# Gating the turns of the next batch by the MoE position, K ahead of Q, and a later zeroing

## The chip, the cores and the metric

One core of one Trainium2 chip. The metric is device time in microseconds (us) of one execution. Every time quoted is the median of several runs; most executions of a kernel here lie within 1% of their median. The engines are named as in the profile: PE (TensorE), ACT (ScalarE), DVE (VectorE), POOL (GpSimd) and SP (SyncE; SPq is its DMA queue). The granted clock, as the profile reads it, is the share of its full clock at which PE could run. "Chunk n" is the n-th group of 64 rows of the sequence, nine chunks to a batch, 72 in all.

## The reference

Cut to what matters: windowed attention over 8 batches of 8 heads, 576 positions and 64 values per head; its result, reordered to 4608 tokens of 512 values, goes through a two-layer block with a squared ReLU (called MoE in the code).

```python
scores = (q @ k.transpose(0, 1, 3, 2)) / np.sqrt(64)
mask = np.abs(pos[:, None] - pos[None, :]) <= 32
attn = softmax(np.where(mask, scores, -1e9))
x = (attn @ v).transpose(0, 2, 1, 3).reshape(4608, 512)
h = x @ w_in                       # 512 x 2048
r = np.maximum(h, 0.0)
out = (r * r) @ w_out              # 2048 x 512
```

## The kernel before

The program records every operation with its engine, what it reads and writes, a modelled duration and a key. A list scheduler written in Python then runs through modelled time; on each engine it issues the ready operation with the lowest key. What it decides is the order on each engine; the waits are semaphores and run on the chip's own time.

```python
def rec(self, eng, fn, reads=(), writes=(), dma=None, dur=100, key=0.0, move=0, after=(), old=()):
    ...                                   # after: operations that must be scheduled earlier
def schedule(self):
    ...
        t, e = best                       # the engine that can issue first, in modelled time
        while wait[e] and wait[e][0][0] <= t:
            _, i, op = heapq.heappop(wait[e])
            heapq.heappush(pool[e], (op.key, i, op))
        op = heapq.heappop(pool[e])[2]    # lowest key among the ready ones
    ...
```

Batches 0 and 1 are turned (transposed) on PE. From batch 2 on, GpSimd loads Q and K raw, VectorE turns them into a staging tile (1.3 us for 512 columns, 1.6 us for 640), and SyncE's queue carries the staging tiles to their places (the "spread"). There is one staging tile for Q and one for K, and two raw tiles of each. So the last Q turn of batch b frees the raw Q tile, and the Q load of batch b+2 can start then (that of batch 4 started 2.0 us after the turn's end in the kernel before, at 85.67 us, and 0.3 us after it in the changed one, at 86.16 us).

```python
def turn(self, b, t, dh, m0, m1, key, after):
    raw, st, i = self.RAW[t][b % 2], self.ST[t], b % 2
    ...
    self.p.rec("DVE", lambda e: e.transpose(dst, src),
               reads=[("raw", t, i, g) for g in range(4)], writes=[("st", t, dh, m0)], key=key,
               dur=40 + 312 * n, after=after)

def spread(self, b, t, key):              # K: 4 transfers of 144 KB, Q: 8 of 72 KB, on SP
    for dh in range(2):                   # two halves, each after two of the four turns
        ...
def copy_v(self, b, key, s0, s1):         # two transfers of 264 KB on SP, vx<-vd
    ...
# in build(), for b > 1
    for st in range(8):
        t, dh, m = ("q", "k")[st // 4], st // 2 % 2, st % 2
        self.turn(b, t, dh, 5 * m, 5 + 4 * m, 9 * b - LEAD - TOFF + st * TST + (5 if b == 2 else 0),
                  [self.masked[min(9 * b - TREL + st, 9 * b - 1) if b > 2 else 12 + st // 2]])
        if st % 4 == 3:
            self.spread(b, t, 9 * b - LEAD - 9)
    self.copy_v(b, 9 * b - LEAD - 6, 0, 4)
```

In the profile the transposes appear as `kst<-kraw` and `qst<-qraw`, the spreads as `kt<-kst` and `qz<-qst`, the V copies as `vx<-vd`. The first scores of a batch (`sc<-qz,kt`) need all of both spreads. Behind the scores come the product with V (`avp`, A·V), its scaling on DVE (`xr`), the transpose of that on PE (`trp`, `xt`) and the MoE (`ht`, its square `gt`, `outp`).

The softmax here doesn't subtract the row's maximum and nothing guards it: scores larger than these inputs give would overflow.

## Time and profile before

| | before |
|---|---|
| median of 3 runs | 346.15 us (343.3 to 348.79) |
| span of the profiled run | 345.2 us |
| PE busy | 312.3 us, 90% |
| PE waits between 60 and 170 us | 9.0 us |
| granted clock in that profile | 0.97 |

The prediction below shows the page, the stretches and the waits. One more view belongs here, since it matters later: the timeline of the kernel before around the first scores of batch 2. The columns are start, length, engine and line, operation, tiles, count, and in brackets the idle time of the engine just before and what ended it. A line of several instructions gives the length from the first to the last.

```profile
89.25 6.18 SPq L378 DMA_DIRECT2D kt<-kst  x4
...
91.81 1.32 DVE L366 STREAM_TRANSPOSE kst<-kraw 128x512 bf16<-128x512 bf16 x1
93.43 2.40 POOL L307 DMA_DIRECT2D kraw<-in_k_dram  x4 [4.75 <-DVE gt L497]
...
101.07 0.61 PE L411 MATMUL sc<-qz,kt 128*128 128x128 bf16 x8 [1.57 <-DMA kt<-kst]
```

Read it as a chain: the last K turn of batch 2 ends at 91.81 + 1.32 = 93.13 us, the K load of batch 4 starts on GpSimd 0.3 us later, the last K transfers are issued by 95.43 us, and the scores can start only at 101.07 us. From the end of the last turn to the scores it takes 7.9 us. For batch 3 the same distance is 115.41 to 123.57 us, 8.2 us. PE ran out of work about 6 us into each. Where the texts below speak of a halved clock: from 117 to 119 us of this profile the granted clock read 0.50, from 117 to 121 us 0.63.

### The profile page before, as it was taken

The page shows a single profiled execution, that of the slowest core. Times are in us where ns is not written, and L with a number is a line of the kernel's source. Part 1 is how long each engine was busy: PE and PEld are TensorE (multiplying, and loading weights), DVE is VectorE, ACT ScalarE, POOL GpSimd, SP SyncE. Part 2 cuts the span into 40 slices and gives each one's busy share as a digit, 9 for nine tenths or more (in the row PEclk, how much of TensorE's full clock was granted, in tenths as well). Part 3 has the DMA queues.
Part 4 walks back from the last instruction along what each step waited for, and adds up shares of the span by engine and source line. Part 5 has one row for each costly group of instructions (what it writes and reads, how often), then busy time and mean ns, then how long its engine had stood idle before and what let it go on. Part 6 is the DMA issues. An engine that isn't in the chain of part 4 may idle for free.

```text
span 345.2 us, 6957 instructions
## 1 busy us (share of the span) xinstructions
PE 312.3 (90%) x2736; PEld 183.1 (53%) x2736; DVE 204.8 (59%) x468; ACT 180.9 (52%) x349; POOL 82.8 (24%) x130
## 2 busy tenths in 40 slices
PE   1457699999989679998999999999999999999996
PEld 1346398776845345544555555555555555444442
DVE  7634556869949857796886676777544444222200
ACT  2365258883536368555565555555555555544421
POOL 8999115102415424141341111100000000000000
PEclk9995689999999899999999999999999999999999
DMA  8999999965996996987997474542200000010012
GB/s 93 185 192 211 171 149 184 208 79 99 218 213 82 243 145 67 123 122 164 176 207 118 80 167 89 85 127 66 65 32 30 34 30 32 30 61 32 30 61 91
DMA packets 76703, 39.63 MB, mean 115 GB/s; under 512 B 41856, under 2 KB 71168, under 8 KB 76672
## 3 DMA queue, kind: packets, MB, share of 16 engines
q0 software_dynamic: 62272, 18.49, 56.7%
q1 hardware_dynamic: 14400, 20.71, 20.4%
q8 instruction: 21, 0.34, 0.4%
q14 instruction: 10, 0.08, 0.1%
HBM read 36.96 MB, written 9.44 MB: 134 GB/s over the span
## 4 chain that ended last, share of the span: by engine, by line
PE 78%; DVE 10%; DMA 6%; ACT 3%; issue 2%; SPq 0%; ACTq 0%
PE outp L529 32%; PE ht L511 26%; PE ht L488 7%; PE sc L411 5%; DMA kt<-kst 4%; DVE kst L366 3%; PE avp L438 3%; PE trp L467 3%; PE avp L439 3%; DMA vx<-vd 2%; DVE qz L204 2%; ACT qz L292 1%; DVE kt L295 1%; PE sc L276 1%; DVE xr L456 1%
## 5 line engine op out<-in xcount | busy, mean ns | idle before, releaser
L529 PE MATMUL outp<-w,gt 128*128 128x512 bf16 x576 | 144.8, 382 | 0.0
L511 PE MATMUL ht<-xt,w 128*128 128x512 bf16 x448 | 115.2, 383 | 0.2 <-ACT xt L471 0.2
L517 ACT ACTIVATE rt<-ht 128x512 bf16<-128x512 f32 x112 | 67.1, 599 | 69.6 <-PE ht L511 67.1
L529 PEld LDWEIGHTS outp<-w,gt 128*128 128x128 bf16 x576 | 54.2, 98 | 57.6 <-issue 1.6
L519 DVE TENSOR_TENSOR gt<-rt 128x512 bf16<-128x512 bf16 x112 | 46.6, 418 | 43.8 <-ACT rt L517 43.3
L511 PEld LDWEIGHTS ht<-xt,w 128*128 128x128 bf16 x448 | 40.8, 99 | 39.1 <-issue 2.1
L416 ACT ACTIVATE e<-sc 128x512 bf16<-128x512 f32 x72 | 42.4, 599 | 25.3 <-PE sc L411 18.2
L423 DVE TENSOR_TENSOR pt<-e,mask 128x512 bf16<-128x512 bf16 x72 | 30.0, 417 | 43.0 <-ACT e L416 42.7
L313 POOL DMA_DIRECT2D vd<-in_v_dram x32 | 28.8, 909 | 87.2 <-PE avp L439 60.6
L471 ACT ACTIVATE xt<-trp 128x256 bf16<-128x256 bf16 x72 | 27.3, 380 | 21.8 <-PE trp L467 21.6
L411 PE MATMUL sc<-qz,kt 128*128 128x128 bf16 x288 | 28.3, 229 | 8.6 <-DVE kt L295 3.9
L488 PE MATMUL ht<-xt,w 128*128 128x128 bf16 x512 | 34.8, 227 | 0.9 <-ACT rt L494 0.7
L366 DVE STREAM_TRANSPOSE kst<-kraw 128x640 bf16<-128x640 bf16 (+1 forms) x24 | 35.0, 1459 | 0.0
L366 DVE STREAM_TRANSPOSE qst<-qraw 128x640 bf16<-128x640 bf16 (+1 forms) x24 | 34.7, 1461 | 0.0
L536 ACT ACTIVATE oe<-outp 128x512 f32<-128x512 f32 x36 | 21.6, 599 | 23.9 <-PE outp L529 23.9
L488 PEld LDWEIGHTS ht<-xt,w 128*128 128x128 bf16 x512 | 31.4, 102 | 2.9 <-ACT rt L494 0.9
L411 PEld LDWEIGHTS sc<-qz,kt 128*128 128x128 bf16 x288 | 21.0, 103 | 18.4 <-DVE kt L295 4.0
L456 DVE TENSOR_TENSOR xr<-avp,rs 128x256 bf16<-128x256 f32 x72 | 30.0, 416 | 0.7
L467 PE MATMUL trp<-ident,xr 128*128 128x128 bf16 x144 | 20.6, 226 | 9.4 <-DVE xr L456 9.4
L454 DVE RECIPROCAL rs<-avp 128x4 f32<-128x4 f32 x72 | 13.4, 186 | 23.6 <-PE avp L439 22.9
L494 ACT ACTIVATE rt<-ht 128x512 bf16<-128x512 f32 x32 | 19.0, 598 | 13.2 <-PE ht L488 11.4
L467 PEld LDWEIGHTS trp<-ident,xr 128*128 128x128 bf16 x144 | 12.5, 99 | 20.9 <-DVE xr L456 10.9
(47 smaller groups left out, 226.1 us busy)
## 6 DMA issues: line engine op xcount, KB each, us to landing
out_dram<-oe SPq DMA_DIRECT2D x36, 256.0 KB, 2.0
vd<-in_v_dram POOLq DMA_DIRECT2D x32, 128.0 KB, 6.3
qraw<-in_q_dram POOLq DMA_DIRECT2D x24, 144.0 KB, 6.9
kraw<-in_k_dram POOLq DMA_DIRECT2D x24, 144.0 KB, 7.3
qz<-qst SPq DMA_DIRECT2D x48, 72.0 KB, 2.6
kt<-kst SPq DMA_DIRECT2D x24, 144.0 KB, 4.2
vx<-vd SPq DMA_DIRECT2D x12, 264.0 KB, 5.9
w<-in_moe_w_in_dram POOLq DMA_DIRECT2D x4, 512.0 KB, 11.6
```

What stands on the lines that cost most here:

```text
L313: self.p.rec("POOL", lambda e, s=s: e.dma_start(self.VD[i][:, s, :, 0:64], v[b, :, 32 + 128 * s:160 + 128 * s, :].rearrange("h p d -> p h ...
L366: self.p.rec("DVE", lambda e: e.transpose(dst, src), reads=[("raw", t, i, g) for g in range(4)], writes=[("st", t, dh, m0)], key=key, dur= ...
L411: mm = e.matmul(sc[:, 128 * j:128 * j + 128], self.KT[i][:, j, 64 * c:64 * c + 128], self.QZ[i][:, j, :, 64 * c:64 * c + 64], start=True, ...
L416: self.p.rec("ACT", lambda e: e.activation(self.E[n % 2][:], sc[:], ACTF.Exp, scale=0.125), reads=[("sc", n % 2)], writes=[("e", n % 2)], ...
L423: self.masked.append(self.p.rec("DVE", lambda e: e.tensor_tensor(pt, ee, mb, ALU.mult), reads=[("e", n % 2), ("mask", mi)], writes=[("pt", ...
L456: self.p.rec("DVE", lambda e: e.tensor_tensor(bass.AP(xr, 0, [[256, 128], [64, 4], [1, 64]]), bass.AP(self.AVP, 0, [[512, 128], [VE, 4], [ ...
L467: mm = e.transpose(self.TRP[:, 128 * t:128 * t + 128], xr[:, 128 * t:128 * t + 128], self.ID[:])
L488: mm = e.matmul(ht[:, 128 * (d % 4):128 * (d % 4) + 128], self.W1[:, ft, 128 * d:128 * d + 128], self.XT[:, ft, t0:t0 + 128], start=(ft == ...
L511: mm = e.matmul(ht[:], self.W1[:, ft, 128 * d:128 * d + 128], self.XT[:, ft, 512 * T:512 * T + 512], start=(ft == 0), stop=(ft == 3))
L517: self.p.rec("ACT", lambda e: e.activation(rt[:], ht[:], ACTF.Relu), reads=[("ht", k % 2)], writes=[("rt", k % 4)], key=key, dur=560)
L519: self.p.rec("DVE", lambda e: e.tensor_tensor(gt[:, d, :], rt[:], rt[:], ALU.mult), reads=[("rt", k % 4)], writes=[("gt", T % 2, d, u) for ...
L529: mm = e.matmul(op[:], gt[:, d, 128 * u:128 * u + 128], self.W2[:, d, :], start=(d == 0), stop=(d == 15))
```

## The change

The intent: turns are held back until the MoE has come to a given block ("gate"), so that they do not run ahead or behind the PE work that is to hide them; K is turned ahead of Q; a zeroing in the start moves behind the first copies. No instruction is added or removed. The core of the diff, with cuts marked:

```diff
-    def rec(self, eng, fn, reads=(), writes=(), dma=None, dur=100, key=0.0, move=0, after=(), old=()):
+    def rec(self, eng, fn, reads=(), writes=(), dma=None, dur=100, key=0.0, move=0, old=(), gate=None, pos=None):
...
+            if op.pos is not None:
+                while held and held[0][0] <= op.pos:
+                    s = heapq.heappop(held)[2]
+                    heapq.heappush(wait[s.eng], (max(s.ready, t), s.i, s))
+                reached = max(reached, op.pos)
...
+                if s.gate is not None and s.gate > reached:
+                    heapq.heappush(held, (s.gate, s.i, s))
+                else:
                     heapq.heappush(wait[s.eng], (s.ready, s.i, s))
...
-                               reads=[tag] + ([w] if par else []), writes=[w], key=key, dur=480)
+                               reads=[tag] + ([w] if par else []), writes=[w], key=key, dur=590)
...
-        self.setup_rest(1, -40)
-        self.setup_qz(1, -30, [(0, 64, 0), (64, 64, 1)])
+        self.setup_rest(1, -6)
+        self.setup_qz(1, -5, [(0, 64, 0), (64, 64, 1)])
...
-                    t, dh, m = ("q", "k")[st // 4], st // 2 % 2, st % 2
-                    self.turn(b, t, dh, 5 * m, 5 + 4 * m, 9 * b - LEAD - TOFF + st * TST + (5 if b == 2 else 0), [self.masked[min(9 * b - TREL + st, 9 * b - 1) if b > 2 else 12 + st // 2]])
+                    t, dh, m = ("k", "q")[st // 4], st // 2 % 2, st % 2
+                    self.turn(b, t, dh, 5 * m, 5 + 4 * m, 9 * b - LEAD - TOFF + st * TST,
+                              9 * b - LEAD - TREL + st if b > 2 else None)
```

The three MoE operations on PE get `pos=key`. The 480 to 590 is only a modelled duration.

More of the change, by code (lines that the diff above doesn't have):

```diff
@@ L29 @@
     __slots__ = ("eng", "fn", "deps", "order", "inc", "val", "sem", "dma", "dur", "key", "i",
-                 "succ", "left", "ready", "start", "end", "lat", "move")
+                 "succ", "left", "ready", "start", "end", "lat", "move", "gate", "pos")
 class Prog:
@@ L45, in __init__ @@
         self.readers = {}
-    def rec(self, eng, fn, reads=(), writes=(), dma=None, dur=100, key=0.0, move=0, after=(), old=()):
+    def rec(self, eng, fn, reads=(), writes=(), dma=None, dur=100, key=0.0, move=0, old=(), gate=None, pos=None):
         op = Op()
         op.eng, op.fn, op.dma, op.dur, op.key, op.move = eng, fn, dma, dur, key, move
-        op.deps, op.order = set(), set(after)
+        op.gate, op.pos = gate, pos
+        op.deps, op.order = set(), set()
         op.inc, op.val, op.sem = False, None, None
@@ L89, in schedule @@
         moved = {"SW": 0, "HW": 0}
-        out = []
+        out, held, reached = [], [], -100
         while True:
@@ L121, in schedule @@
                 s.left -= 1
-                if not s.left:
+                if s.left:
+                    continue
+                if s.gate is not None and s.gate > reached:
+                    heapq.heappush(held, (s.gate, s.i, s))
+                else:
                     heapq.heappush(wait[s.eng], (s.ready, s.i, s))
@@ L292, in fine_turn @@
                     self.p.rec("ACT", lambda e, d=dst, c=src: e.activation(d, c, ACTF.Copy),
-                               reads=[tag] + ([w] if par else []), writes=[w], key=key, dur=480)
+                               reads=[tag] + ([w] if par else []), writes=[w], key=key, dur=590)
                 else:
                     self.p.rec("DVE", lambda e, d=dst, c=src: e.tensor_copy(d, c),
-                               reads=[tag] + ([w] if par else []), writes=[w], key=key, dur=480)
+                               reads=[tag] + ([w] if par else []), writes=[w], key=key, dur=590)
     def load_qk(self, b, t, key):
@@ L358, in load_w2, with turn @@
                    writes=[("w2", d)], dma=(f"w2{d}", 0), key=key, dur=770, move=2700)
-    def turn(self, b, t, dh, m0, m1, key, after):
+    def turn(self, b, t, dh, m0, m1, key, gate):
         raw, st, i = self.RAW[t][b % 2], self.ST[t], b % 2
@@ L367, in turn @@
                    reads=[("raw", t, i, g) for g in range(4)], writes=[("st", t, dh, m0)], key=key,
-                   dur=40 + 312 * n, after=after)
+                   dur=40 + 312 * n, gate=gate)
     def spread(self, b, t, key):
@@ L422, in scores @@
         mb = bass.AP(msk, 0, [[64, 128], [0, 4], [0, 2], [1, 64]])
-        self.masked.append(self.p.rec("DVE", lambda e: e.tensor_tensor(pt, ee, mb, ALU.mult),
-                                      reads=[("e", n % 2), ("mask", mi)], writes=[("pt", n % 2)], key=key, dur=430))
+        self.p.rec("DVE", lambda e: e.tensor_tensor(pt, ee, mb, ALU.mult),
+                   reads=[("e", n % 2), ("mask", mi)], writes=[("pt", n % 2)], key=key, dur=430)
     def av(self, n):
@@ L492, in mm1_small @@
         self.p.rec("PE", f, reads=[("xt", 8 * T + 2 * g), ("xt", 8 * T + 2 * g + 1), ("w1", q)], writes=[("ht", k % 2)], key=key,
-                   dur=900)
+                   dur=900, pos=key)
         self.p.rec("ACT", lambda e: e.activation(rt[:], ht[:], ACTF.Relu), reads=[("ht", k % 2)],
@@ L515, in mm1 @@
         self.p.rec("PE", f, reads=[("xt", 8 * T + j) for j in range(8)] + [("w1", d // 4)], writes=[("ht", k % 2)],
-                   key=key, dur=864)
+                   key=key, dur=864, pos=key)
         self.p.rec("ACT", lambda e: e.activation(rt[:], ht[:], ACTF.Relu), reads=[("ht", k % 2)],
@@ L532, in mm2 @@
         self.p.rec("PE", f, reads=[("gt", T % 2, d, u) for d in range(4 * seg, 4 * seg + 4)] + [("w2", seg)],
-                   writes=[("outp", x % 2)], key=key, dur=864)
+                   writes=[("outp", x % 2)], key=key, dur=864, pos=key)
         if seg == 3:
@@ L543, in build @@
         self.k1 = 0
-        self.masked = []
         K = -100.0
```

## The prediction

> **What bounds the kernel now.** I read the page first, then the busy time by stretches of a few microseconds, then the waits of PE alone, then PE's and DVE's timelines inside the stretches that lose time, and last the order in which the two built programs issue their instructions. From the page:
>
> ```profile
> span 345.2 us, 6957 instructions
> PE 312.3 (90%) x2736; PEld 183.1 (53%) x2736; DVE 204.8 (59%) x468; ACT 180.9 (52%) x349; POOL 82.8 (24%) x130
> PE   1457699999989679998999999999999999999996
> PEclk9995689999999899999999999999999999999999
> ```
>
> PE is the bound: 312.3 of 345.2 us. Both programs issue the same matrix work (72 attention chunks, 288 MoE blocks of some 0.87 us each), so the change can only remove PE's idle time (33 us) or the time at a halved clock. Stretches of the run (columns: stretch, length, busy us of PE, PEld, DVE, ACT, POOL with counts, PE clock, DMA share, GB/s):
>
> ```profile
> 72.00:98.00 26.00, 26.00 (x309) 18.69 (x307) 23.08 (x39) 12.73 (x25) 7.15 (x11) 1.00 0.81 141
> 98.00:102.00 4.00, 2.43 (x18) 1.22 (x17) 0.00 (x0) 1.11 (x3) 0.00 (x0) 1.00 1.17 283
> 110.00:117.00 7.00, 3.22 (x50) 2.21 (x48) 6.76 (x13) 3.25 (x8) 3.19 (x5) 0.97 1.35 228
> 117.00:121.00 4.00, 4.00 (x13) 1.49 (x12) 2.73 (x6) 1.19 (x2) 1.47 (x3) 0.63 1.50 226
> 121.00:125.00 4.00, 1.90 (x24) 1.30 (x23) 1.19 (x5) 1.60 (x4) 0.89 (x1) 1.00 1.44 216
> 150.00:160.00 10.00, 8.95 (x62) 4.51 (x60) 7.03 (x9) 5.54 (x10) 2.41 (x4) 1.00 1.01 212
> 160.00:330.00 170.00, 170.00 (x1182) 87.84 (x1180) 92.83 (x215) 91.23 (x177) 14.23 (x20) 1.00 0.38 77
> ```
>
> After 160 us PE never idles, so nothing is to be had there. Some 21 us of idle time lie in the first 40 us. The part that the turns can touch is 98 to 160 us: 1.57 + 3.78 + 2.10 + 1.05 = 8.5 us idle. PE's waits between 60 and 160 us say for whom (us in total, times, longest):
>
> ```profile
> PE trp L467 <- DVE xr L456: 4.1, 4, 1.6
> PE sc L411 <- DMA kt<-kst: 3.7, 2, 2.1
> PE avp L438 <- DMA vx<-vd: 1.0, 1, 1.0
> ```
>
> At 112 to 116 us DVE runs a K turn between every two chunks while PE has no MoE block left to fill with:
>
> ```profile
> 112.01 1.60 DVE L366 STREAM_TRANSPOSE kst<-kraw 128x640 bf16<-128x640 bf16 x1
> 113.42 0.19 DVE L454 RECIPROCAL rs<-avp 128x4 f32<-128x4 f32 x1
> 113.45 0.41 DVE L423 TENSOR_TENSOR pt<-e,mask 128x512 bf16<-128x512 bf16 x1
> 113.78 0.40 DVE L456 TENSOR_TENSOR xr<-avp,rs 128x256 bf16<-128x256 f32 x1
> 116.81 4.30 PE L511 MATMUL ht<-xt,w 128*128 128x512 bf16 x12 [0.23 <-ACT xt L471]
> ```
>
> The last K turn of batch 3 ends at 115.4, its spread reaches kt only at 123.5 (2.10 us idle).
>
> [...] after 110 to 117 us at 46% busy, 12 matmuls took 4.30 us at clock 0.63, where 20 of the same size took 4.48 us at 95 us; 12 at that pace are 2.6 us, so 1.7 us were lost beside the idle time. [...] a turn placed ahead of an xr holds that xr, and then PE, for the turn's whole length; the trace shows a cadence of 1.40 us (640 columns) and 1.11 us (512). [...] a qz spread lands after 2.5 us (median of the four issued at 106 us) or 5.3 us (four at 119 us, beside the next K load), a kt spread after 2.5 us (142 us) or 7.2 us (three at 114 us).
>
> **The change part by part.** It adds and removes no instruction; everything is order.
>
> *Zeroing of the second Q buffer.* One of the two 64-row memsets (1.02 us, with its gap 1.3 us) moves behind the first kt copies; the other stays ahead. Before: copies from 8.86, first scores at 11.34 us, 3.9 us waiting for kt. After: scores some 1.25 us earlier. But at 25.62 us PE waits 2.6 us for work from the V copies, whose issue (19.23 us) hangs on a POOL load that was issued at 8.69 us and does not move. I book 0 us.
>
> *Batch 2.* Its turns lose the "+5" in the key and the masks; K goes first (one Q turn stays ahead). MoE blocks issued before the first scores of batch 2: 56 before, 47 after; nine blocks (7.8 us) are kept to fill later gaps. The price, walked along DVE: between xr of chunk 16 and xr of chunk 17 now stand a 640 turn, rs, and a 512 turn: 1.40 + 0.10 + 1.11 + 0.42 = 3.0 us, while PE has only one transpose pair and one A·V (0.35 us): 2.65 us idle. One chunk earlier a turn costs 0.2 us. Then PE has 2 large and 3 small blocks (4.4 us); the last Q turn ends 0.4 us before they start, and its four spreads take 1.9 us to issue and 2.6 to 5.3 us to land, so the scores wait 0 to 2.4 us; I take 1.0. Sum 3.9 us, against 1.57 us before.
>
> *Batch 3.* The K turns come among chunks 18 to 20, each beside 2 to 3 MoE blocks; chunks 20 to 26, which had no filler before, now have 1 to 3 blocks between them (1.7 us and more, against DVE's 0.8 us for rs, mask and xr plus at most 1.4 us for a turn). Before: 3.78 us of starving, 2.10 us for kt and 1.7 us of half clock. After: 0.3 us for xt, and for the Q spread, with 6 blocks (5.9 us) between the last Q turn and the scores against 4.7 to 7.4 us, 0 to 1.6 us; I take 0.6. Gain 7.6 − 0.9 = 6.7 us.
>
> *Batch 4.* The last turn comes one chunk earlier, but one pair of MoE blocks (1.7 us) is gone between it and the scores, and the V copy now stands in SP's queue behind four Q spreads (2.5 us to issue) instead of two K spreads (1.25 us). Before, the V copy issued at 152.68 us was ready near 159.7 us, 1.0 us late. After, I count the V copy at about the same distance from the last chunk of batch 3, and PE 1.7 us sooner there, of which 0.8 us I give back for the earlier turn: 1.9 us idle, a loss of 0.9 us.
>
> *Sum.* Before: 8.5 idle + 1.7 half clock = 10.2 us. After: 3.9 + 0.9 + 1.9 = 6.7 us, and 0.3 us for the chance that the 2.65 us gap lets the clock fall. Gain 3.2 us: 346.15 − 3.2 = 343.0 us.
>
> **The rivals.**
> *A: the turns take their own place.* All spreads land at the slow figures (5.3 us) and the gap at chunk 17 is followed by a halved clock: batch 2 costs 5.3 + 1.7, batch 3 1.9, batch 4 3.1 us, in sum 12.0 us; the time would be 348 us. For it: the Q and K loads of the batch after next are still released by the last turn and so still meet the spread. Against it: the many spreads that landed in under 3 us.
> *B: everything is hidden.* The nine kept blocks cover all, the gap at chunk 17 alone remains (2.65 us): gain 7.5 us, 338.6 us. For it: batches 5 to 7 never idle before, and their spreads have 4 chunks' room. Against it: the DVE order at chunk 17 is plain.
> *C: the start gains too.* If the first 1.25 us survive, 341.8 us. Against it: the wait at 25.62 us hangs on a transfer, and POOL is busy without a break from 10 to 30 us.
> *D: DVE becomes the bound.* 23.1 of 26 us before 98 us, but 55% after 160 us, and no work is added; it costs nothing beyond the walk above.
>
> **Range and chances.** My walk has about ±3 us in it (transfers 2, clock 1.7, start 1), and the three runs before spread by ±2.7 us. So 343.0 us, 338.5 to 347.5 us. Faster by over 2% needs less than 339.2 us, which is rival B whole or B with C: 0.15. Slower by over 2% needs 353 us, more than rival A: 0.03. The rest: 0.82.
>
> **What would show it right or wrong.** Right: PE's wait for xr at chunk 17 of some 2.6 us, near 75 to 80 us; no starving between chunks 20 and 26 and no clock of 0.5 to 0.6 after 60 us; first scores at about 10.1 us but the A·V of chunk 2 still at about 25.6 us; a wait for the V copy of 1 to 3 us at the first A·V of batch 4; no idle time after batch 5 begins. Wrong: idle PE below 3 us between 60 and 170 us (B), the kt waits back under the name of qz at over 2 us each with a fallen clock (A), or A·V of chunk 2 ahead of 25 us (C).

## The result, and the profile after

After: 356.97 us, median of 4 runs (355.32 to 357.65). Before, with one more run beside it: 346.44 us (343.3 to 348.79). The ratio is 1.0328, 95% interval 1.0246 to 1.041: slower. Of the four before, the one of 348.79 us lies 1.6% above the fastest, counts as slow and stays out of the ratio (356.73 / 345.40). A ratio here is the mean time of one kernel's fast runs over that of the other's of the same rounds, so it is not quite the ratio of the medians. In microseconds, 3.28% of 346.4 is 11.4 us.

The page of the changed kernel, span, busy times, PE's row and the granted clock in 40 slices, and the group of the scores:

```profile
span 353.6 us, 6914 instructions
...
PE 311.7 (88%) x2696; PEld 185.5 (52%) x2736; DVE 207.6 (59%) x468; ACT 181.5 (51%) x349; POOL 82.8 (23%) x130
...
PE   1477699996499939999899999999999999999996
...
PEclk9999999999879987999999999999999999999999
...
L423 PE MATMUL sc<-qz,kt 128*128 128x128 bf16 x288 | 28.9, 237 | 15.7 <-DMA qz<-qst 12.1
```

PE's busy time is the same as before (311.7 against 312.3 us; some matmul records are missing). The loss shows as two holes in PE's row, at the 11th and the 15th slice, each with a lower clock in it and behind it. The group of the scores waited 15.7 us, where it waited 8.6 us before. PE's waits between 60 and 170 us (us in total, times, longest):

```profile
PE sc L423 <- DMA qz<-qst: 12.1, 3, 6.1
PE trp L479 <- DVE xr L468: 2.8, 2, 2.4
PE avp L450 <- DMA vx<-vd: 1.4, 1, 1.4
```

The kt wait of before (3.7 us) is gone, and a wait for Q three times as long has come. The stretches around both holes (stretch, length, busy us of PE, PEld, DVE, ACT, POOL with counts, PE clock, DMA share, GB/s):

```profile
84.00:91.00 7.00, 4.56 (x57) 3.58 (x58) 4.68 (x11) 3.15 (x6) 3.10 (x6) 1.00 1.41 227
91.00:97.00 6.00, 0.74 (x9) 0.66 (x8) 0.61 (x1) 0.61 (x2) 0.00 (x0) 0.86 1.13 221
97.00:104.00 7.00, 7.00 (x87) 7.00 (x85) 5.07 (x9) 3.24 (x6) 0.59 (x1) 0.63 0.19 45
...
125.00:132.00 7.00, 0.89 (x8) 0.73 (x8) 1.30 (x3) 0.67 (x2) 0.20 (x1) 0.82 1.09 151
132.00:138.00 6.00, 5.95 (x34) 3.09 (x34) 2.77 (x9) 3.74 (x8) 0.58 (x1) 0.64 0.00 0
```

In the holes (91 to 97 and 125 to 132 us) every compute engine is nearly idle (PE busy for 0.74 of 6 and 0.89 of 7 us) and the DMA engines are full (DMA share 1.13 and 1.09). Behind each hole PE is busy but at 0.63 and 0.64 of its clock; read by single microseconds the clock was 0.50 from 97 to 102 and from 132 to 136 us. The timeline at the first hole says what came when:

```profile
84.58 1.29 DVE L378 STREAM_TRANSPOSE qst<-qraw 128x512 bf16<-128x512 bf16 x1
...
85.46 0.52 SPq L350 DMA_DIRECT2D vx<-vd  x1
...
86.03 0.60 SPq L358 DMA_DIRECT2D vx<-vd  x1
...
86.16 2.48 POOL L319 DMA_DIRECT2D qraw<-in_q_dram  x4 [1.48 <-DVE xr L468]
...
86.18 0.28 PE L479 MATMUL trp<-ident,xr 128*128 128x128 bf16 x2 [2.37 <-DVE xr L468]
...
86.67 4.41 SPq L398 DMA_DIRECT2D qz<-qst  x4
...
96.34 1.03 PE L423 MATMUL sc<-qz,kt 128*128 128x128 bf16 x8 [5.26 <-DMA qz<-qst]
```

The last Q turn of batch 2 ends at 85.87 us. The last four transfers of its spread are not issued then: two V copies of 264 KB stand ahead of them in the same queue, so the first goes at 86.67 us. At 86.16 us GpSimd starts the Q load of batch 4, which that very turn has set free. With both running, the issue of the four transfers takes 4.41 us, and the last lands 5.3 us later. From the end of the last turn to the scores: 0.8 + 4.4 + 5.3 = 10.5 us, where before took 7.9 us. PE ran out of work 5.2 us into it. The second hole has the same lines:

```profile
117.55 1.31 DVE L378 STREAM_TRANSPOSE qst<-qraw 128x512 bf16<-128x512 bf16 x1
...
119.43 0.51 SPq L350 DMA_DIRECT2D vx<-vd  x1
...
119.45 2.42 POOL L319 DMA_DIRECT2D qraw<-in_q_dram  x4 [1.49 <-DVE xr L468]
...
120.63 4.31 SPq L398 DMA_DIRECT2D qz<-qst  x4
...
131.28 1.04 PE L423 MATMUL sc<-qz,kt 128*128 128x128 bf16 x8 [6.11 <-DMA qz<-qst]
```

At batch 3 it is 1.8 + 4.3 + 6.3 = 12.4 us (118.86 to 131.28) against 8.2 us, and PE ran out of work after 6.3 us.

### The profile page after: what moved, and what is told of

Read it like the earlier page. It is cut to its first block, busy times and chain, and to the rows that moved or that the text cites.

```text
span 353.6 us, 6914 instructions
## 1 busy us (share of the span) xinstructions
PE 311.7 (88%) x2696; PEld 185.5 (52%) x2736; DVE 207.6 (59%) x468; ACT 181.5 (51%) x349; POOL 82.8 (23%) x130
## 4 chain that ended last, share of the span: by engine, by line
PE 80%; DMA 8%; DVE 4%; ACT 3%; SPq 2%; issue 2%; POOL 1%; POOLq 0%
PE outp L541 32%; PE ht L523 26%; PE ht L500 8%; PE sc L423 5%; DMA qz<-qst 4%; PE avp L450 3%; DMA vx<-in_v_dram 2%; PE trp L479 2%; PE avp L451 2%; SPq L398 2%; DMA vx<-vd 2%; ACT qz L304 1%; PE sc L288 1%; DVE gt L509 1%; DVE qst L378 1%
## 5 line engine op out<-in xcount | busy, mean ns | idle before, releaser
L541 PE MATMUL outp<-w,gt 128*128 128x512 bf16 x557 | 139.3, 379 | 1.2 <-DVE gt L509 0.3
L523 PE MATMUL ht<-xt,w 128*128 128x512 bf16 x427 | 112.0, 384 | 1.7 <-ACT xt L483 0.6
L541 PEld LDWEIGHTS outp<-w,gt 128*128 128x128 bf16 x576 | 53.4, 98 | 56.9 <-DVE gt L509 0.2
L523 PEld LDWEIGHTS ht<-xt,w 128*128 128x128 bf16 x448 | 41.4, 99 | 41.4 <-issue 1.7
L423 PE MATMUL sc<-qz,kt 128*128 128x128 bf16 x288 | 28.9, 237 | 15.7 <-DMA qz<-qst 12.1
L500 PE MATMUL ht<-xt,w 128*128 128x128 bf16 x512 | 36.8, 235 | 0.9 <-ACT rt L506 0.6
L500 PEld LDWEIGHTS ht<-xt,w 128*128 128x128 bf16 x512 | 33.6, 107 | 2.4 <-ACT rt L506 1.1
L506 ACT ACTIVATE rt<-ht 128x512 bf16<-128x512 f32 x32 | 18.9, 596 | 11.5 <-PE ht L500 11.3
L479 PEld LDWEIGHTS trp<-ident,xr 128*128 128x128 bf16 x144 | 12.4, 99 | 18.6 <-DVE xr L468 9.7
```

The lines of the kernel that those rows point to most:

```text
L423: mm = e.matmul(sc[:, 128 * j:128 * j + 128], self.KT[i][:, j, 64 * c:64 * c + 128], self.QZ[i][:, j, :, 64 * c:64 * c + 64], start=True, ...
L479: mm = e.transpose(self.TRP[:, 128 * t:128 * t + 128], xr[:, 128 * t:128 * t + 128], self.ID[:])
L500: mm = e.matmul(ht[:, 128 * (d % 4):128 * (d % 4) + 128], self.W1[:, ft, 128 * d:128 * d + 128], self.XT[:, ft, t0:t0 + 128], start=(ft == ...
L523: mm = e.matmul(ht[:], self.W1[:, ft, 128 * d:128 * d + 128], self.XT[:, ft, 512 * T:512 * T + 512], start=(ft == 0), stop=(ft == 3))
L541: mm = e.matmul(op[:], gt[:, d, 128 * u:128 * u + 128], self.W2[:, d, :], start=(d == 0), stop=(d == 15))
```

## The experiments

The theory after the result: the last half of the Q spread comes late because it (A) stands behind two V copies and shares the DMA engines with them, and (B) shares the DMA engines with loads that the turns set free. (In the profile after, from 86 to 92 us, the packets of GpSimd's loads took 90.7% of the 16 DMA engines' span and those of SyncE's transfers 49.2%.) The rival theories: the order of the turns itself costs; the later zeroing costs; or the clock does. In most experiments the scheduler's order is kept on every engine (`reorder`), and one edit is then made in one queue, so that the order on the other engines stays; e7, e8 and e14 are scheduled afresh, and more can move. There is no e3. Each kernel computed the right result. Ratios are to the kernel before, on the same chip and in the same rounds. At a threshold of 2% the verdict is unclear for e5 and e13, there is none for e7, and it is "same" for all others, so that gains and losses of about 1% are read from the intervals.

**e1: the zeroing alone, on the kernel before.**

```diff
-        self.setup_rest(1, -40)
-        self.setup_qz(1, -30, [(0, 64, 0), (64, 64, 1)])
+        self.setup_rest(1, -6)
+        self.setup_qz(1, -5, [(0, 64, 0), (64, 64, 1)])
```

> The kernel before with the zeroing of the second Q buffer moved behind the first copies, and nothing else. Theory (the loss is in the turns and spreads of batches 2 to 4): within 1% of before, about 346 us; first scores at about 10.1 us instead of 11.3, the A.V of chunk 2 still at about 25.6 us. Rival (the move at the start does the harm): over 350 us.

Measured: 346.16 us, ratio 1.0001 (0.9961 to 1.0042). The zeroing is worth nothing either way, as the prediction had it.

**e2: the changed kernel, V copies of batches 2 and 3 ahead of their K spread.**

```diff
+        sp = queue["SP"]
+        for b in (2, 3):
+            v = ...   # the two V copies of batch b, taken out of SP's queue
+            x = sp.index(kq[0])           # the first transfer of the K spread of batch b
+            sp[x:x] = v
```

> The changed kernel with every engine's order kept, but the two V copies of batches 2 and 3 moved on the SP queue from between the two halves of the Q spread to ahead of the K spread. Theory A (the V copies stand ahead of the last four Q spreads in SP's queue[...]): the waits of the first scores of batches 2 and 3 for qz fall from 5.3 and 6.1 us to about 2 and 2.5 us, the halved clock behind them goes, 345 to 349 us. Theory B (the raw loads on the POOL queue slow the spread): each wait falls by no more than the 1.2 us that the two V copies take to issue, about 354 us.

Measured: 345.94 us, ratio 0.9983 (0.9948 to 1.0019): the whole loss is gone. The issue of batch 2's Q spread, and PE's wait for it from 40 to 180 us:

```profile
83.88 6.16 SPq L413 DMA_DIRECT2D qz<-qst  x8
```
```profile
PE sc L438 <- DMA qz<-qst: 4.1, 2, 2.4
```

The V copies of batch 2 went out at 74.42 us, ahead of the K spread, so the eight Q transfers follow each other without a break. At batch 3 the last four are issued in 2.54 us from 115.13 us. Two waits for Q, of 2.35 and 1.76 us, remain.

**e4: the changed kernel, the Q and K loads of batches 4 and 5 held until the first scores of batches 2 and 3.** The V copies stay where they were.

```diff
+        for o in queue["POOL"]:
+            if o.dma and o.dma[0] in ("q0", "q1", "k0", "k1") and o.dma[1] in (4, 5):
+                o.deps.add(self.sc_op[9 * (o.dma[1] - 2)])
```

> The changed kernel with every engine's order kept, but the K loads of batches 4 and 5 on the POOL queue (and by the order of that queue what stands behind them: V and Q loads) wait for the first scores of batches 2 and 3. Theory B (raw loads beside the spread): the waits for qz fall from 5.3 and 6.1 us to under 2 us, 345 to 349 us. Theory A (V copies): they stay at 4 to 6 us, 354 to 357 us.

Measured: 342.5 us, ratio 0.9892 (0.9811 to 0.9972): more than the loss. The issue of the last four Q transfers of batch 2, the load that now starts behind the scores, the wait that is left, and the Q spreads in the DMA view from 70 to 135 us (last number: median us to landing):

```profile
88.19 3.10 SPq L413 DMA_DIRECT2D qz<-qst  x4
...
95.50 2.42 POOL L334 DMA_DIRECT2D kraw<-in_k_dram  x4 [21.11 <-PE sc L438]
```
```profile
PE sc L438 <- DMA qz<-qst: 0.5, 1, 0.5
```
```profile
qz<-qst SPq DMA_DIRECT2D x16, 72.0 KB, 2.1
```

In the changed kernel the last of these lines reads 5.9 us instead of 2.1.

**e5: e2 and e4 together.** The edit is the sum of both.

> e2 and e4 together. Both theories: the waits for qz under 1 us, no halved clock after 60 us, and what is left is the 2.4 us at chunk 17 and the wait at the first chunks of batch 4: about 342 us. If the waits stay above 3 us, neither V copies nor loads are the cause, but the issue of the spreads itself.

Measured: 341.85 us, ratio 0.988 (0.979 to 0.997; 4 runs). The two cures do not add: by the medians 11.0 us and 14.5 us alone, 15.1 us together.

**e6: the kernel before, with the late loads of e4 only.**

> The kernel before with every engine's order kept, but the Q and K loads of batches 4 and 5 (and by POOL's order what stands behind them) wait for the first scores of batches 2 and 3. If loads beside a spread slow it in any order: the waits for kt fall from 3.7 us in sum to under 1 us, 341 to 345 us. If only the changed order suffers from them: about 346 us. Beside e4 and e5 it tells what the changed order is worth when its spreads are left alone: same as e4 within 1% if the order itself gains nothing.

Measured: 342.15 us, ratio 0.9858 (0.9809 to 0.9908). PE no longer waits for kt. The starving between chunks 20 and 26 stays (3.8 us for xr). So with the loads out of the way the old order is as fast as the new one: 342.15 against 342.5 us.

**e8: the changed kernel with Q turned ahead of K**, that is, the gates without the exchange. The edit swaps the pair ("k", "q") back; the scheduler then runs afresh.

> The changed kernel with Q turned ahead of K again, rescheduled; the scheduler now puts the V copies between the two halves of the K spread. If the place of the V copies beside the loads costs: waits for kt of 3 to 6 us at the first scores of batches 2 and 3, 350 to 357 us. If K ahead of Q costs: about 346 us.

Measured: 347.98 us, ratio 1.0054 (1.0012 to 1.0096). The scheduler now puts the V copies between the two halves of the K spread. Batch 2 waits as long as ever:

```profile
97.76 1.01 PE L423 MATMUL sc<-qz,kt 128*128 128x128 bf16 x8 [5.82 <-DMA kt<-kst]
```

and batch 3 only 1.92 us, so the result lies between the two expectations. The long wait at batch 2 is not bound to the exchange of Q and K. In both batches the V copies had been issued just before the last turn ended (87.38 against 87.62 us, 119.83 against 120.68 us), so the last K transfers did not stand behind them. What differs is the load: in batch 2 the K load of batch 4 starts 0.3 us after that turn, and from the turn to the scores it takes 10.1 us; in batch 3 the load starts 2.4 us after it, and it takes 7.4 us.

**e7 and e14: the kernel before, K turned ahead of Q only** (the same kernel, run twice).

```diff
-                    t, dh, m = ("q", "k")[st // 4], st // 2 % 2, st % 2
+                    t, dh, m = ("k", "q")[st // 4], st // 2 % 2, st % 2
```

> The kernel before with K turned ahead of Q and nothing else (masks and the +5 stay); the V copies come ahead of all Q spreads of batch 2. If the order of K and Q is what costs (four Q spreads come last instead of two K spreads): over 352 us with waits for qz of 4 us and more. If the place of the V copies and the lost room cost: 345 to 350 us.

> The kernel before with K turned ahead of Q and nothing else, timed again since the first look gave no ratio (4 runs from 344.4 to 351.5 us). If the order of K and Q is by itself the cause: 355 us or more, 2.5% above before. If it only costs together with the gates and the nine MoE blocks kept back: 346.5 to 349 us, 0.2 to 0.8% above.

Measured: e7 gave 348.85 us in 4 runs (344.43 to 351.46), two of them slow (over 1.5% above its fastest), and no ratio. e14, 22 runs: 347.15 us, ratio 1.0033 (1.0006 to 1.006). Its profile has three waits for Q, the longest 1.9 us. At batch 3 the V copies went out at 106.46 us, ahead of the whole Q spread. The exchange alone costs a third of a per cent.

**e9: the kernel before, V copies between the halves of the K spread** in batches 2 and 3, the place that they have in the changed kernel.

> The kernel before with every engine's order kept but SP's: the V copies of batches 2 and 3 moved from ahead of the K spread to between its two halves, as in the changed kernel. If that place costs by itself: waits for kt up from 3.7 us to 6 to 10 us in sum, 349 to 354 us. If it costs nothing without the rest of the change: within 1% of 346 us.

Measured: 347.26 us, ratio 1.0033 (1.0001 to 1.0065), where 349 us and more were expected if the place alone did the harm: a miss for that form of theory A. Of PE's two waits for kt the first stays (1.56 us, before 1.57) and the second grows from 2.10 to 3.21 us; neither comes near the 5 to 6 us of the changed kernel. The V copies were all issued about 1 us before the last turn ended here (90.71 against 91.80 us, 113.09 against 114.06 us), so they never held the last K transfers back.

**e10: the changed kernel, V copies behind the whole Q spread.**

> The changed kernel with every engine's order kept but SP's: the V copies of batches 2 and 3 behind the whole Q spread instead of between its halves. If it is the copies ahead in the queue that hold the Q spread back: the waits for qz fall as in e2 (5.3 and 6.1 us to 2 to 3 us), and the first A.V of each batch waits for V instead, 1 to 4 us each; 347 to 352 us. If the place in the queue does not matter and only the bytes in flight do: waits for qz of 4 us and more.

Measured: 347.47 us, ratio 1.0046 (1.0021 to 1.007). By the medians it recovers 9.5 us. The waits for Q at batches 2 and 3 are 1.46 and 2.20 us (the third, at batch 4, makes up the sum), and the V copies are now waited for (2.6 us in two waits):

```profile
PE sc L438 <- DMA qz<-qst: 4.6, 3, 2.2
```

**e11: the changed kernel, only the Q loads of batches 4 and 5 late.**

> The changed kernel with only the Q loads of batches 4 and 5 waiting for the first scores of batches 2 and 3; the K loads and the V load between them stay early. If the loads that the last Q turn releases do the harm: waits for qz under 2.5 us each, 343 to 347 us. If the K and V loads issued some 5 us before the last turn do it: waits of 3 to 5 us, 348 to 353 us.

Measured: 345.95 us, ratio 0.9994 (0.9964 to 1.0023). The waits for Q fall to 1.38 and 0.37 us:

```profile
PE sc L438 <- DMA qz<-qst: 1.7, 2, 1.4
```

So the loads that the last Q turn itself sets free (and what stands behind them in GpSimd's queue) are needed for the loss: the K and V loads before them, beside the V copies, do not make it.

**e12: e5, and the last Q turn of batch 2 behind the xr of chunk 17, and the V copy of batch 4 ahead of its Q spread.**

> The version that the runs point to: e5 (V copies first, loads late), with the last Q turn of batch 2 moved behind xr of chunk 17 (takes 1.1 of the 2.4 us of waiting there) and the V copy of batch 4 ahead of its Q spread (takes the 1 to 2 us at its first A.V). From e5's 341.9 us minus 2 to 3 us: 339 to 340 us, faster than both kernels; if other waits take their place, 342 us.

Measured: 341.07 us, ratio 0.9885 (0.9838 to 0.9932; 4 runs). Not below e5 by more than the scatter: the wait at chunk 17 fell to 1.5 us and the V wait went, but a wait of PE for gt (1.6 us) and one for Q (1.4 us) took their places. A miss.

**e13: the changed kernel, with idle work in the two long waits.** 18 matmuls that nothing reads stand ahead of the first scores of batches 2 and 3. The spread is left as it is; only PE's clock is to be kept up.

```diff
+        for n in (18, 27):
+            op = Op()                     # a PE operation with the scores' waits, but for the DMAs
+            op.fn = lambda e, n=n: self.fill(e, self.SC[n % 2])
+            x = pe.index(self.sc_op[n])
+            pe[x:x] = [op]
+    def fill(self, e, sc):
+        for _ in range(18):
+            mm = e.matmul(sc[:], self.ID[:], self.W1[:, 0, 0:512], start=True, stop=True)
+        return mm
```

> The changed kernel with 18 matmuls of 512 columns that nothing reads (3.9 us at full clock) put on PE directly ahead of the first scores of batches 2 and 3, inside the two waits of 5.3 and 6.1 us for the Q spread; results stay right and the spreads are untouched. Theory (some 6 us of the loss are the halved clock[...]): the waits left are 1.4 and 2.2 us, the stretches after them run at full clock, and the time falls by 5 to 6 us to 351-352 us, 1.4 to 1.8% above the kernel before. Rival (the clock costs nothing of its own, the loss is the late spread alone): the scores start when the data lands and the time stays at 356-358 us.

Measured: 353.41 us (351.08 to 356.0, 4 runs), ratio 1.0209 (1.0153 to 1.0265). Against 1.0328 for the changed kernel that is 1.19%, or 4.1 us; the theory had expected 5 to 6, and the two intervals just touch (1.0246 to 1.0265). The profile shows it in the clock. The stretches of the changed kernel that stood at 0.63 and 0.64, here:

```profile
97.00:104.00 7.00, 6.24 (x106) 5.82 (x108) 6.31 (x10) 4.45 (x8) 0.59 (x1) 1.00 0.25 48
...
132.00:138.00 6.00, 5.95 (x60) 3.64 (x60) 4.72 (x13) 5.32 (x11) 1.46 (x2) 1.00 0.28 18
```

The clock is 1.00, and in the same 7 and 6 us PE's records rise from 87 and 34 to 106 and 60. The scores still start late: 97.71 us and 129.74 us.

**All runs in one sum.** For each profile, between 60 and 170 us: all of PE's waits added up; the time lost to the clock, as the sum over stretches of 6 us (the last of 8) of PE's busy time times one minus the granted clock; for e13 also the 3.83 + 4.05 us of idle work. The last two columns compare the total with that of before, and with the measured ratio (its part over 1, times 346.4 us).

| kernel | waits | clock | total | over before | measured |
|---|---|---|---|---|---|
| before | 9.0 | 1.2 | 10.2 | | |
| after | 17.2 | 5.3 | 22.5 | +12.3 | +11.4 |
| e1 zeroing only | 9.5 | 1.2 | 10.7 | +0.5 | 0.0 |
| e2 V first | 9.8 | 0 | 9.8 | -0.4 | -0.6 |
| e4 loads late | 6.5 | 1.3 | 7.8 | -2.4 | -3.7 |
| e5 both | 5.5 | 0 | 5.5 | -4.7 | -4.2 |
| e6 before, loads late | 5.1 | 2.4 | 7.5 | -2.7 | -4.9 |
| e7 K first only | 8.8 | 2.7 | 11.5 | +1.3 | no ratio |
| e8 Q first | 11.9 | 2.0 | 13.9 | +3.7 | +1.9 |
| e9 before, V between | 10.2 | 1.4 | 11.6 | +1.4 | +1.1 |
| e10 V last | 11.2 | 3.6 | 14.8 | +4.6 | +1.6 |
| e11 Q loads late | 7.2 | 1.1 | 8.3 | -1.9 | -0.2 |
| e12 all three | 5.5 | 2.6 | 8.1 | -2.1 | -4.0 |
| e13 fill | 8.7 + 7.9 | 0 | 16.6 | +6.4 | +7.2 |
| e14 K first only | 9.0 | 1.5 | 10.5 | +0.3 | +1.1 |

A single profile agrees with the timed runs within 3 us, and for most within 2: it is one run of a kernel whose runs spread by 5 us. The large terms stand out from that: after has 8.2 us more of waits and 4.1 us more of lost clock than before, and e13 takes away 4.1 us.

## Why the prediction was wrong, and where it was right

The prediction was 343.0 us with a range up to 347.5 us; 356.97 us came. The chance given to what came was 0.03.

**Right.** The idle time at chunk 17 is 2.37 us (said: 2.65): the xr that PE waits for started at 85.67 us, behind a 640 and a 512 turn (83.14 and 84.58 us). In the kernel before, PE waited 1.57 us for an xr behind one 640 turn and 1.28 us behind one 512 turn (ending at 114.25 and 116.05 us). First scores come at 10.13 us (said: about 10.1), the A·V of chunk 2 at 25.41 us (said: about 25.6), and the whole time gains nothing from it (e1). The starving between chunks 20 and 26 is gone: the waits for xr fall from 4.1 to 2.8 us, of which 2.37 are those of chunk 17. At batch 4 a Q wait of 0.68 and a V wait of 1.4 us make 2.1 us (said: 1.9, but all of it for V, so the sum fits partly by luck). After batch 5 begins there is no idle time.

**Wrong: the landing of the Q spread.** The steps that failed read "its four spreads take 1.9 us to issue and 2.6 to 5.3 us to land, so the scores wait 0 to 2.4 us" for batch 2, and, for batch 3, "against 4.7 to 7.4 us, 0 to 1.6 us; I take 0.6". Measured, from the end of the last turn: 10.5 and 12.4 us, so waits of 5.26 and 6.11 us where 1.0 and 0.6 were booked. Three parts of that term were mis-sized:

- The start: the V copies of batches 2 and 3 stand ahead in SP's queue (0.8 and 1.8 us). The prediction saw this place for batch 4 only. In the order of the changed program it could be read beforehand.
- The issue: the 1.9 us runs to the start of the last transfer; so counted it took 3.8 and 3.7 us (4.4 and 4.3 us to its end), with two V copies and the freed loads under way. e4, with the loads gone, has 3.10 us to its end, and in a quiet place (84.04 us) 2.62 us, 0.65 us a transfer. Even there the four spent more time on issue than one on landing (2.1 us).
- The landing: 5.8 and 6.9 us from the start of the last transfer (5.3 and 6.3 us from its end), where 2.6 to 5.3 us were expected. In e4 the median of the same four at batch 2 is 2.7 us.

The profile of before held the warning: its own last spread of a batch took 7.9 and 8.2 us from the last turn to the scores, beside the same kind of load. The prediction took its landing times from other places of the trace and set them together without the queue; the 7.2 us of the K spread at 114 us, which it had read at just such a place, did not enter. The distance of 7.9 and 8.2 us, taken as it stood, would have given waits of 2.7 and 1.9 us even without the V copies.

**Wrong: the clock.** "0.3 us for the chance that the 2.65 us gap lets the clock fall" was booked, an estimate of the author's; 4.1 us more than before were lost, behind the two waits and not at chunk 17. e13, which takes away the fallen clock and leaves the late spread, gains 4.1 us, though its interval touches that of the changed kernel. Waits of 5.26 and 6.11 us were followed by clocks of 0.63 and 0.64; in e2, with waits of 2.4 us at most, the clock stayed at 1.00 from 60 to 170 us. But one long wait is not the only way to lose it, and the chance that was booked was a real one: in e4 the clock was at 0.82 from 84 to 91 us, around the idle time of 2.46 us at chunk 17, in e12 at 0.75 from 84 to 90 us, where no wait passed 1.6 us, and in e10 at 0.52 from 126 to 132 us, where the waits were 2.20 and 1.21 us and PE was busy for 3.80 us of the 6 before. In the trace of before, too, the clock of 0.63 from 117 to 121 us came without a long wait: in the stretch of 110 to 117 us PE was busy for 3.22 of 7 us, and its longest wait was 1.57 us. (By the prediction's own figures the loss there is 1.6 us, not 1.7: 12 matmuls at the pace of 20 in 4.48 us take 2.7 us.)

**Rival A** had the direction, with slow landings and a fallen clock, but at 5.3 + 1.7 us for batch 2 and 1.9 us for batch 3 it came to 348 us. By its walk these 5.3 us are the idle time at chunks 16 and 17 (2.85) and a wait for Q of 2.4 us. Measured were 2.4 + 0.3 + 5.3 us and 3.0 us of clock at batch 2, 10.9 us in all, and 0.6 + 6.1 us and 2.3 us of clock at batch 3, 9.0 us. Both were too small, batch 3 by most.

**What is shown, and what is not.** Shown: both the V copies (e2, e10) and the freed loads (e4, e11) are needed for the loss; taking away either brings both waits to 2.4 us or less, and 9.5 to 14.5 us of the medians come back. From the last Q turn of batch 2 to the scores it took 7.6 us in e2, 8.0 in e10 and 8.1 in e11, as in the kernel before (7.9), against 10.5 us. It fits with this that the cures do not add (e5), and that the parts alone cost 0.0, 0.3 and 0.5% (e1, e14, e8) but 3.3% together. Shown as well: once the loads are late, neither order is clearly better (e4 against e6). Shown in the profile, but in time only with intervals that touch: the 4.1 us of the clock. Open: how far the V copies harm by their place in the queue and how far by their share of the DMA engines. e9 has them between the halves without the loss, but there they went out early enough to hold nothing back, and with K's larger transfers; e10 has them behind, where they still share. Batch 2 of e8 has a long wait (5.82 us) with nothing held back in the queue, which speaks for the sharing, but its whole order is another. Open as well: how much PE work within a stretch keeps the clock up, since e13 tried one amount. Open too is why the clock in the first 60 us differs from run to run: the profile of before had it at 5 and 6 tenths in places where the one of after had it full, and that may be why the profiled spans differ by 8.4 us where the waits and the clock past 60 us differ by 12.3.

The best versions seen are e12, e5, e6 and e4, at 341.07 to 342.5 us, 1.1 to 1.4% under the kernel before. That is inside 2%; e6 has the smallest edit to the kernel before.

## What to carry to other kernels

When a step frees a buffer, ask what load that starts, and whether it meets the transfer that the same step has just made ready; holding that load until the consumer has started was worth 4 us to the old order and 14 to the new. Take the time of such a transfer from the end of its producer to the start of its consumer at the same place of the old trace, with the queue and its neighbours in it, rather than adding an issue time and a landing time from quieter places. And look at every PE wait that may grow to several microseconds: those of 5.3 and 6.1 us cost the clock behind them as well (0.63 and 0.64, some 4 us), so delays that are harmless alone can together cost more than their sum.
